# Two of the seven products of a Strassen-like layer made by halves again, in two of three chunks

## The chip, the cores and the metric

The kernel runs on one core of one Trainium2 chip. The metric is the device time of one execution in microseconds (us). The kernel before takes 889.53 us, the median of 3 runs (889.41 to 889.66). The profile is of one such execution; its span is 887.6 us.

The engines are named as the profile names them: PE is TensorE (matmul), PEld its weight load, DVE is VectorE, ACT is ScalarE, POOL is GpSimd, SP is SyncE. A queue name such as SPq or POOLq stands for the transfers that this engine issues.

## The reference

The reference is an attention with a mask, followed by a feed-forward part with a squared ReLU. The change touches the feed-forward part only.

```python
# attention: batch 4, heads 8, sequence 768, head_dim 64
attn_out = hash_attention(q, k, v, proj)           # masked softmax, cut here
# bridge: (B,H,S,D) -> (B*S, H*D) = (3072, 512)
x = attn_out.transpose(0, 2, 1, 3).reshape(B * S, H * D)
# feed-forward: w_in (512, 2048), w_out (2048, 512), all f32
h = x @ w_in
r = np.maximum(h, 0.0)
g = r * r
out = g @ w_out
```

## The kernel before

The kernel works in two parts. The first, up to about 335 us, does the attention and writes its result to `x_all`. The second does the feed-forward part in 3 chunks of 1024 tokens. In each chunk there is a first layer (`h = x @ w_in` and the gate) and a second layer (`g @ w_out`, called `project`).

Both layers save matmuls by a scheme of Strassen's kind. A product of 2 x 2 blocks, which would need eight block products, is made of seven: four of the seven factors on each side are sums or differences of blocks, and the results are added up. The first layer applies the scheme once. A unit is 2 x 128 rows of hidden features (blocks `b11`, `b12`, `b21`, `b22`), and there are 8 units a chunk. The second layer applies the scheme twice, which makes 49 products with factors called `leaf`. All factors on the weight side are prepared earlier and kept in device memory: `w_in_7` for the first layer, `w_out_49` for the second.

The seven products, shared by both layers. Each `add` is a group of `n` matmuls into an accumulator in PSUM; three of the outputs share an accumulator, whose running value is copied out between the products:

```python
def product(n, w, at, bt, c11, c12, c21, c22, hook=None):
    acc = [ps_m.tile([P, 512], FP32, name=f"acc{i}")[:, 0:w] for i in range(3)]
    ...                                   # add(), keep(): keep copies acc out by ScalarE
    add(0, at(0), bt["11"], True, False)
    one = keep(0, "one")
    add(1, at(1), bt["21"], True, True)
    if hook:
        hook()
    c11(acc[1], one)
    add(0, at(4), bt["t2"], False, False)
    two = keep(0, "two")
    add(2, at(3), bt["t1"], True, False)
    five = keep(2, "five")
    add(0, at(5), bt["t3"], False, False)
    three = keep(0, "three")
    add(2, at(6), bt["22"], False, True)
    c12(acc[2], two)
    c22(three, five)
    add(0, at(2), bt["t4"], False, True)
    c21(acc[0])
```

The first layer. `HN` is 512 columns, `NFT // 2` is 2 tiles of the contraction:

```python
def load_unit(n, pool=p_i):               # 7 factors of a unit, 896 KB, on SP's queue
    r = n % NR
    w_unit[n] = pool.tile([P, 7, NFT // 2, P], FP32, name="w_unit", bufs=2 ...)
    nc.sync.dma_start(out=w_unit[n], in_=w_in_7[r])

def hidden(i, r):
    ...
    def gate(out):
        def put(one, two=None):
            h = p_r.tile([P, HN], FP32, name="h", bufs=NH)
            if two is None:
                nc.scalar.copy(out=h, in_=one)
            else:
                nc.vector.tensor_tensor(out=h, in0=one, in1=two, op=ALU.add)
            nc.vector.scalar_tensor_tensor(
                out=out[:, r], in0=h, scalar=0.0, in1=h, op0=ALU.max, op1=ALU.mult
            )
        return put
    product(NFT // 2, HN, lambda a: lambda f: w[:, a, f], bt,
            gate(b11), gate(b12), gate(b21), gate(b22))
```

The second layer, cut to its order. `QN` is 256 columns, `NQ` is 4. Seven outer products `k`, each made by a `product` of seven inner ones with 4 matmuls of 256 columns. The operand `y21` of an inner seventh product is made in place by `hook`, on DVE. Sums of the next outer factor are made ahead by `inner_sums`:

```python
for k in range(7):
    ...
    def hook():
        y21 = b[:, NQ:NR, 0:QN]
        minus(y21, y21, t2)
        if k + 1 < 7 and k not in (1, 3):
            inner_sums(k + 1)
    product(NQ, QN, a_with_load, bt, ..., hook)
    if k == 0 and i + 1 < NCHUNK:
        load_x(i + 1)                      # 2048 KB on POOL's queue
    if k in (3, 4) and i + 1 < NCHUNK:
        sum_x(i + 1, 2 * k - 5); sum_x(i + 1, 2 * k - 4)
    if k == 0:                             # k == 2 alike, with b_t and b21
        for h in range(2): minus(b11[...], b22[...], b_t[...])
        inner_sums(2)
```

The main loop, cut. `peak` is a maximum over 768 elements a row of `q` and `k` that the kernel needs once; its 32 pieces are spread over chunks 2 and 3:

```python
for i in range(NCHUNK):
    for r in range(NR):
        hidden(i, r)
        minus(b_t[:, r], b12[:, r], b11[:, r])
        ...                                # work on w_out's factors in chunk 1
        load_unit(i * NR + r + ...)
        for n in range(2):
            m = 2 * ((i - 1) * NR + r) + n
            if m >= 0: peak(m)
            if 0 <= m + 2 < NPK: load_peak(m + 2)
        if r >= THEN[-1]:                  # r >= 5
            inner_sums(0, slice(r - NQ if r > THEN[-1] else 0, r - NQ + 1))
        minus(b12[:, r], b22[:, r], b12[:, r])
    project(i)
```

Of the kernel before, what the change touches and what calls it, by code (L numbers as in the profile page):

```python
# [8 lines left out]
FP32 = mybir.dt.float32  # L9
# [25 lines left out]
def kernel(  # L35
# [10 lines left out]
    nc = tc.nc  # L46
# [34 lines left out]

    HF, HD, NR, NQ = DFF // 2, DM // 2, NFF // 2, NFF // 4
    w_in_7 = p_d.tile([NR, P, 7, NFT // 2, P], FP32, name="w_in_7")
    w_in_21 = p_d.tile([P, NFT // 2, HF], FP32, name="w_in_21")
    w_out_1 = p_d.tile([P, NFF, DM], FP32, name="w_out_1")
    w_out_49 = p_d.tile([7, P, 7, NQ, P], FP32, name="w_out_49")
# [110 lines left out]
    def put_factor(n, c, t):  # L197

        for f in range(NFT // 2):
            rs = t[:, f].rearrange("p (r c) -> p r c", c=P)  # L200
            nc.sync.dma_start(
                out=w_in_7[c // P:c // P + rs.shape[1], :, n, f].rearrange("r p c -> p r c"), in_=rs
            )


# [298 lines left out]

    def sums_a(a11, a12, a21, a22, s1, s2, s3, s4):
        nc.vector.tensor_tensor(out=s1, in0=a21, in1=a22, op=ALU.add)
        nc.vector.tensor_tensor(out=s3, in0=a11, in1=a21, op=ALU.subtract)
        nc.vector.tensor_tensor(out=s2, in0=s1, in1=a11, op=ALU.subtract)  # L510
        nc.vector.tensor_tensor(out=s4, in0=a12, in1=s2, op=ALU.subtract)

    def minus(out, in0, in1):
        nc.vector.tensor_tensor(out=out, in0=in0, in1=in1, op=ALU.subtract)  # L514
# [28 lines left out]

    w_unit = {}

    def load_unit(n, pool=p_i):

        if n < NCHUNK * NR and n not in w_unit:
            r = n % NR
            w_unit[n] = pool.tile([P, 7, NFT // 2, P], FP32, name="w_unit", bufs=2 if pool is p_i else 1)  # L550
            nc.sync.dma_start(out=w_unit[n], in_=w_in_7[r])

    def sum_x(i, n):

# [18 lines left out]
    with tc.manual_schedule():  # L573
# [191 lines left out]
                op0=ALU.mult, op1=ALU.is_gt,  # L765
            )

        def hidden(i, r):

            x, t_x = xs[i]  # L770
            lo, hi = slice(0, HN), slice(HN, NCH)
            w = w_unit.pop(i * NR + r)
            bt = {
                "11": lambda f: x[:, f, lo], "21": lambda f: x[:, 2 + f, lo],
                "22": lambda f: x[:, 2 + f, hi], "t4": lambda f: x[:, f, hi],
            }
            for n in range(3):
                bt[f"t{n + 1}"] = lambda f, n=n: t_x[n][:, f]

            def gate(out):  # L780
                def put(one, two=None):
                    h = p_r.tile([P, HN], FP32, name="h", bufs=NH)
                    if two is None:
                        nc.scalar.copy(out=h, in_=one)
                    else:
                        nc.vector.tensor_tensor(out=h, in0=one, in1=two, op=ALU.add)  # L786
                    nc.vector.scalar_tensor_tensor(  # L787
                        out=out[:, r], in0=h, scalar=0.0, in1=h, op0=ALU.max, op1=ALU.mult
                    )
                return put  # L790

            product(
                NFT // 2, HN, lambda a: lambda f: w[:, a, f], bt, gate(b11), gate(b12), gate(b21),
                gate(b22),
            )

        def parts_t(b, n):

            lo, hi = slice(0, QN), slice(QN, HN)
            return b[:, n, lo], b[:, n, hi], b[:, NQ + n, lo], b[:, NQ + n, hi]  # L800


        OUTER = (0, b11), (5, b12), (3, b_t), (6, b22), (1, b21), (4, b11), (2, b_t)
# [3 lines left out]
        def inner_sums(k, n=slice(0, NQ)):  # L807

            if k not in tens:
                tens[k] = [p_y.tile([P, NQ, QN], FP32, name=f"t{m}", bufs=2) for m in range(2)]  # L810
            t1, t2 = (t[:, n] for t in tens[k])
            b = OUTER[k][1]
            at = slice(NQ + n.start, NQ + n.stop)
            y11, y12, y21, y22 = b[:, n, 0:QN], b[:, n, QN:HN], b[:, at, 0:QN], b[:, at, QN:HN]
            minus(t1, y12, y11)
            minus(t2, y22, t1)
            minus(y12, y22, y12)
# [3 lines left out]
        def load_leaf(n, early=False):  # L821
            if n < 49:
                k, m = divmod(n, 7)
                m = LEAVES[m]
                leaves[k, m] = p_y.tile([P, NQ, P], FP32, name="leaf", bufs=NLEAF)
                queue = nc.sync if early else nc.scalar
                queue.dma_start(out=leaves[k, m], in_=w_out_49[OUTER[k][0], :, m])
# [55 lines left out]
        def project(i):  # L883
# [54 lines left out]
            def fourth(n, one, two):  # L938
                add_to(out_block(1, 0, n), block(W, n), whole(one, two))
                close(1, 0, n)  # L940

            uses = first_, seventh, fifth, third, second, sixth, fourth
            for k in range(7):
                b = OUTER[k][1]
                t1, t2 = tens.pop(k)
                at = lambda m, k=k: lambda n: leaves[k, m][:, n]
                bt = {
                    "11": lambda n: b[:, n, 0:QN], "21": lambda n: b[:, NQ + n, 0:QN],
                    "22": lambda n: b[:, NQ + n, QN:HN], "t1": lambda n: t1[:, n],
                    "t2": lambda n: t2[:, n], "t3": lambda n: b[:, n, QN:HN],  # L950
                    "t4": lambda n: b[:, NQ + n, 0:QN],
                }

                def hook():
                    y21 = b[:, NQ:NR, 0:QN]
                    minus(y21, y21, t2)
                    if k + 1 < 7 and k not in (1, 3):
                        inner_sums(k + 1)

                counted = []  # L960

                def a_with_load(m, k=k):
                    load_leaf(7 * k + len(counted) + NLEAF - 2)
                    counted.append(m)
                    return at(m)

                use = uses[k]
                product(
                    NQ, QN, a_with_load, bt, lambda *p: use(0, *p), lambda *p: use(1, *p),
                    lambda p: use(2, p, None), lambda *p: use(3, *p), hook,  # L970
                )
                if k == 0 and i + 1 < NCHUNK:
                    load_x(i + 1)
                if k in (3, 4) and i + 1 < NCHUNK:
                    sum_x(i + 1, 2 * k - 5)
                    sum_x(i + 1, 2 * k - 4)
                if k == 5 and i + 1 == NCHUNK:
                    guard()
                if k == 0:

                    for h in range(2):
                        at_h = slice(h * NQ, (h + 1) * NQ)
                        minus(b11[:, at_h], b22[:, at_h], b_t[:, at_h])
                    inner_sums(2)
                if k == 2:

                    for h in range(2):
                        at_h = slice(h * NQ, (h + 1) * NQ)
                        minus(b_t[:, at_h], b21[:, at_h], b11[:, at_h])
                    inner_sums(4)  # L990
# [41 lines left out]
        load_unit(2, p_1)  # L1032
        load_rows(1)
        for i in range(NCHUNK):
            for r in range(NR):
                hidden(i, r)
                minus(b_t[:, r], b12[:, r], b11[:, r])
                if i == 0 and r in WHEN:
                    sums_out(WHEN.index(r))
                if i == 0 and r in THEN:  # L1040
                    m = THEN.index(r)
                    sums_out_49(m)
                    if m + 2 < NQ:
                        load_rows(m + 2)
                if i == 0 and r == THEN[-1]:
                    p_1s.close()
                    p_y = fast.enter_context(tc.tile_pool(name="p_y", bufs=1, reuse_waits="tile"))
                load_unit(i * NR + r + (3 if i == 0 and r < 2 else 2))
                if r == NR - 2:
                    for n in range(NLEAF - 2):  # L1050
                        load_leaf(n, i == 0)
                for n in range(2):
                    m = 2 * ((i - 1) * NR + r) + n
                    if m >= 0:
                        peak(m)
                    if 0 <= m + 2 < NPK:
                        load_peak(m + 2)
                if r >= THEN[-1]:
                    inner_sums(0, slice(r - NQ if r > THEN[-1] else 0, r - NQ + 1))
                minus(b12[:, r], b22[:, r], b12[:, r])  # L1060
            if i == NCHUNK - 1:
                tops()
            project(i)
# [5 lines left out]
def general(tc, slow, ident, w_in_7, w_in_21, w_out_1, q, k, v, proj, out_v):  # L1069
# [19 lines left out]
    with ExitStack() as stack:  # L1089
# [9 lines left out]
        with tc.If(flag > 0), ExitStack() as inner:  # L1099
            const = inner.enter_context(tc.tile_pool(name="g_const", bufs=1))  # L1100
            w_out = const.tile([P, NFF, DM], FP32, name="g_w_out")
            nf, nr = NFT // 2, NFF // 2
            for n, f, c in (0, 0, 0), (1, nf, 0), (2, nf, nr):
                for i in range(nf):
                    nc.sync.dma_start(
                        out=w_in_d[c:c + nr, :, f + i], in_=w_in_7[:, :, n, i]
                    )
# [192 lines left out]
```

## Time and profile before

| what | value |
|---|---|
| time, median of 3 | 889.53 us (889.41 to 889.66) |
| span of the profiled execution | 887.6 us |
| mean granted PE clock | 0.997 of full speed |
| HBM traffic | 119.28 MB read, 38.01 MB written |
| `w_unit<-w_in` loads | 24 of 896 KB, median 4.7 us to landing |
| `leaf<-w_out` loads on ACT's queue | 142 of 256 KB, median 2.9 us to landing |

How to read it. The page gives the busy time of each engine, the span in 40 slices, the DMA queues, the chain of work that ended last (followed back from the last instruction), and groups of instructions by source line. A group names the tile that is written and those that are read, `acc<-x,w_unit`, with the shape and the count. A timeline line has the start, the duration, the engine, the source line and the operands, and in brackets how long the engine was idle before and who released it. A matmul in f32 appears as two records, and its modelled end can lie after the start of the next one, so the spacing of the starts tells more than the durations. Line 697 is the matmul in `add`, line 514 the helper `minus`.

### The profile page before, as it was taken

How to read it: one execution, taken by the hardware profiler on the slowest of the kernel's cores; microseconds unless marked ns; L12 is line 12 of the kernel's file. 1: busy time of each engine (PE TensorE's matmuls, PEld its weight loads, DVE VectorE, ACT ScalarE, POOL GpSimd, SP SyncE). 2: the span in 40 equal slices, each digit the busy share in tenths (PEclk: the TensorE clock that was granted, in tenths of full speed). 3: DMA queues.
4: the chain of work that ended last, by engine and by line, in shares of the span. 5: the costliest groups of instructions: out<-in, count | busy, mean ns of one | idle time of the engine just before them, and what ended most of it. 6: DMA issues, size and time to landing. Idle time of an engine off the chain costs nothing.

```text
span 887.6 us, 11727 instructions
## 1 busy us (share of the span) xinstructions
PE 873.3 (98%) x4268; PEld 502.7 (57%) x4268; DVE 715.8 (81%) x994; ACT 376.0 (42%) x609; POOL 91.5 (10%) x148
## 2 busy tenths in 40 slices
PE   8999999999999999999999999999999999999996
PEld 3444444444444444444688854445888644458885
DVE  5899999999999998888779955568789556778875
ACT  5988888888888852222111112222111122221110
POOL 2000000000000001554000111112000111100002
PEclk9999999999999999999999999999999999999998
DMA  9677779898878536999855834447757444444565
GB/s 182 130 150 134 196 184 202 167 277 198 167 154 213 155 114 222 293 264 292 312 169 152 190 85 137 132 152 259 255 162 176 74 154 154 153 132 145 163 172 104
DMA packets 220032, 158.14 MB, mean 178 GB/s; under 512 B 163808, under 2 KB 180704, under 8 KB 219968
## 3 DMA queue, kind: packets, MB, share of 16 engines
q1 hardware_dynamic: 186848, 84.04, 39.3%
q10 hardware_dynamic: 22384, 37.76, 14.1%
q0 software_dynamic: 10736, 35.53, 13.2%
q8 instruction: 35, 0.57, 0.3%
q14 instruction: 29, 0.24, 0.1%
HBM read 119.28 MB, written 38.01 MB: 177 GB/s over the span
## 4 chain that ended last, share of the span: by engine, by line
PE 93%; DVE 4%; ACT 1%; DMA 1%; issue 1%; ACTq 0%; DVEq 0%
PE acc L697 60%; PE st L394 17%; PE xo L436 13%; PE tot L455 2%; PE hash L344 1%; DVE total L426 1%; DMA k_nat<-in_k_dram 1%; ACT e L411 1%; ACT bits L354 1%; DVE peaks L738 0%; DVE b L787 0%; DVE h L786 0%; DMA w_in<-s_in 0%; DVE t L514 0%; DVE out_piece L177 0%
## 5 line engine op out<-in xcount | busy, mean ns | idle before, releaser
L697 PE MATMUL acc<-x,w_unit 128*128 128x512 f32 x384 | 169.4, 593 | 0.0
L411 ACT ACTIVATE e<-st 128x1024 f32<-128x1024 f32 x192 | 145.2, 810 | 46.9 <-PE st L394 42.7
L394 PE MATMUL st<-feat,feat 64*128 64x512 f32 (+1 forms) x768 | 150.5, 484 | 0.0
L436 PE MATMUL xo<-e,v_nat 128*64 128x512 f32 (+1 forms) x768 | 134.8, 492 | 0.0
L697 PE MATMUL acc<-b,leaf 128*128 128x256 f32 x600 | 132.9, 380 | 0.0
L697 PE MATMUL acc<-t_x,w_unit 128*128 128x512 f32 x288 | 127.6, 593 | 0.0
L697 PEld LDWEIGHTS acc<-x,w_unit 128*128 128x128 f32 x384 | 73.0, 190 | 90.5 <-issue 88.5
L697 PEld LDWEIGHTS acc<-b,leaf 128*128 128x128 f32 x600 | 114.3, 190 | 16.5 <-issue 1.4
L426 DVE TENSOR_TENSOR total<-total,e 128x1536 f32<-128x1536 f32 x61 | 107.1, 1756 | 4.3
L436 PEld LDWEIGHTS xo<-e,v_nat 128*64 128x64 f32 x768 | 51.4, 136 | 82.4 <-issue 75.2
L697 PEld LDWEIGHTS acc<-t_x,w_unit 128*128 128x128 f32 x288 | 54.8, 190 | 69.0 <-issue 66.8
L394 PEld LDWEIGHTS st<-feat,feat 64*128 64x128 f32 x768 | 66.1, 188 | 33.7 <-issue 24.1
L786 DVE TENSOR_TENSOR h<-acc,two 128x512 f32<-128x512 f32 x24 | 16.6, 691 | 83.7 <-PE acc L697 83.6
L704 ACT COPY two<-acc 128x512 f32<-128x512 f32 (+1 forms) x45 | 21.9, 486 | 132.6 <-PE acc L697 132.6
L697 PE MATMUL acc<-t,leaf 128*128 128x256 f32 x336 | 76.5, 380 | 0.3 <-DVE t L514 0.3
L354 ACT ACTIVATE bits<-hash,lifts 32x384 bf16<-32x384 f32 x120 | 68.6, 572 | 3.2 <-issue 1.3
L697 PEld LDWEIGHTS acc<-t,leaf 128*128 128x128 f32 x336 | 63.8, 190 | 9.5 <-DVE t L514 1.1
L704 ACT COPY one<-acc 128x512 f32<-128x512 f32 (+1 forms) x45 | 21.9, 486 | 111.8 <-PE acc L697 78.3
L787 DVE SCALAR_TENSOR_TENSOR b<-h 128x512 f32<-128x512 f32 x96 | 64.3, 690 | 2.5
L394 PE MATMUL st<-bits,bits 64*128 64x256 bf16 (+1 forms) x384 | 63.3, 326 | 1.8 <-ACT e L411 1.4
L697 PE MATMUL acc<-b_t,leaf 128*128 128x256 f32 x240 | 53.8, 380 | 0.0
L697 PEld LDWEIGHTS acc<-b_t,leaf 128*128 128x128 f32 x240 | 45.6, 191 | 6.1
(130 smaller groups left out, 864.3 us busy)
## 6 DMA issues: line engine op xcount, KB each, us to landing
leaf<-w_out ACTq DMA_DIRECT2D x142, 256.0 KB, 2.9
w_unit<-w_in SPq DMA_DIRECT2D x24, 896.0 KB, 4.7
raw<-in_moe_w_in_dram SPq DMA_DIRECT2D x16, 512.0 KB, 5.6
raw<-in_moe_w_out_dram SPq DMA_DIRECT2D x16, 512.0 KB, 4.3
w_out<-sums POOLq DMA_DIRECT2D x16, 448.0 KB, 6.8
v_nat<-in_v_dram SPq DMA_DIRECT2D x16, 384.0 KB, 4.9
x_all<-x_t SPq DMA_DIRECT2D x16, 384.0 KB, 3.0
x<-x_all POOLq DMA_DIRECT2D x3, 2048.0 KB, 12.2
```

What stands on the lines that cost most here:

```text
L344: nc.tensor.matmul(out=banks[g * NR_B:(g + 1) * NR_B, h, 0:HS], lhsT=projs[rows], rhs=feat[pr, w][rows, c * HS:(c + 1) * HS], start=True, ...
L354: nc.scalar.activation(out=t[h * D:h * D + NR_B, c * HS:(c + 1) * HS], in_=hashed[pr, w][at, h, 0:HS], func=ACTF.Sign, scale=HUGE, bias=li ...
L394: nc.tensor.matmul(out=st[:, h, 0:hi - lo], lhsT=src[pr, 1][rows, key], rhs=src[pr, 0][rows, lo:hi], start=first, stop=not first,)
L411: nc.scalar.activation(out=e[:, :, lo:hi], in_=sts[i][:, :, 0:hi - lo], func=ACTF.Exp, scale=scale)
L426: nc.vector.tensor_tensor(out=totals[pr], in0=totals[pr], in1=weights[pr, kt][:, :, 0:S], op=ALU.add)
L436: nc.tensor.matmul(out=xo[h * D:(h + 1) * D, lo:hi], lhsT=nat[pr, "v_nat"][:, h, kt * D:(kt + 1) * D], rhs=weights[pr, kt][:, h, lo:hi], s ...
L455: nc.tensor.matmul(out=tot[g * 32:(g + 1) * 32, 0:HS], lhsT=ones, rhs=src[:, h, c * HS:(c + 1) * HS], start=src is srcs[0], stop=src is sr ...
L697: nc.tensor.matmul(out=acc[to], lhsT=a(i), rhs=b(i), start=first and i == 0, stop=last and i == n - 1, skip_group_check=True,)
L704: nc.scalar.copy(out=t, in_=acc[of])
L786: nc.vector.tensor_tensor(out=h, in0=one, in1=two, op=ALU.add)
L787: nc.vector.scalar_tensor_tensor(out=out[:, r], in0=h, scalar=0.0, in1=h, op0=ALU.max, op1=ALU.mult)
```

## The change

In the second and third chunk, the units of the first layer are taken in pairs (units n and n + 4). Five of the seven products stay as they are for each unit. The other two, those with factors 1 and 2 of each unit, are joined over the pair: two units by two tiles of the contraction are a 2 x 2 block on the weight side, and the 512 columns are cut in two on the other side. Each of the two is then made by the scheme again: seven inner products of one matmul of 256 columns, in place of two units by two matmuls of 512 columns. This is for fewer matmul columns: 7 x 256 in place of 8 x 256 for each.

The weight factors for it, `w_in_49`, are made from `w_in_7` during the second layer of the first chunk, with loads and stores on POOL's queue and sums on DVE. The order of the factors in `w_in_7` changes so that the five that stay lie together. The matmuls of an inner product stand between those of the outer ones, so that the copy of an accumulator has time. The partial results go to snapshot tiles in place of output tiles that are free then (`o`), and the inner factors go to tiles of the second layer that are free then (`sum0` to `sum3`, `t0`, `t1`). The maxima `peak` move to the end of a unit's work, behind the inner sums.

```diff
+    w_in_49 = p_d.tile([NQ, P, 2, 7, P], FP32, name="w_in_49")
...
+    PLACE = 0, 5, 6, 1, 2, 3, 4
...
-            r = n % NR
+            r = order(n)                       # units 0,4,1,5,2,6,3,7 from chunk 2 on
             w_unit[n] = pool.tile([P, 7, NFT // 2, P], FP32, name="w_unit", ...)
-            nc.sync.dma_start(out=w_unit[n], in_=w_in_7[r])
+            m = 7 if n < NR else 5
+            nc.sync.dma_start(out=w_unit[n][:, 0:m], in_=w_in_7[r, :, 0:m])
...
+        def factor_units(n):                   # second layer of chunk 1, k = 0..3
+            src = [new_h()... for _ in range(2)]
+            for j in range(2):
+                nc.gpsimd.dma_start(out=src[j], in_=w_in_7[j * NQ + n, :, 5:7])
+            sums = [new_h()... for _ in range(2)]
+            sums_a(...)                        # 4 DVE operations of 256 elements a row
+            for lo, hi, t in (...):            # 4 stores
+                nc.gpsimd.dma_start(out=w_in_49[n, :, :, lo:hi], in_=t)
+
+        def load_inner(i, n):                  # 2 loads of 448 KB a pair, on SP's queue
+            ...
+        def sums_inner(i):                     # 8 DVE operations of 256, once a chunk
+            ...
+        def inner_steps(i, n, j):
+            ...
+            def step_0():
+                a0, a1 = (ps_m.tile([P, 512], FP32, name="acc1")[:, 0:QN] for _ in range(2))
+                mul(a0, 0, y11, True, False)
+                nc.scalar.copy(out=one, in_=a0)
+                mul(a1, 1, y21, True, True)
+                hs[0] = new_h()
+                nc.vector.tensor_tensor(out=hs[0][:, 0:QN], in0=a1, in1=one, op=ALU.add)
+            def step_1():
+                hs["a2"] = ps_t.tile([P, 512], FP32, name="acc3")[:, 0:QN]
+                mul(hs["a0"], 4, t[:, 1], False, False)
+                nc.scalar.copy(out=two, in_=hs["a0"])
+                mul(hs["a2"], 3, t[:, 0], True, False)
+                nc.scalar.copy(out=five, in_=hs["a2"])
+            def step_2():
+                mul(hs["a0"], 5, t3, False, False)
+                nc.scalar.copy(out=three, in_=hs["a0"])
+                mul(hs["a2"], 6, y22, False, True)
+                nc.vector.tensor_tensor(out=hs[0][:, QN:HN], in0=hs["a2"], in1=two, op=ALU.add)
+                hs[1] = new_h()
+                nc.vector.tensor_tensor(out=hs[1][:, QN:HN], in0=three, in1=five, op=ALU.add)
+            def step_3():
+                mul(hs["a0"], 2, t[:, 2], False, True)
+                nc.scalar.copy(out=hs[1][:, 0:QN], in_=hs["a0"])
+            def put(unit, out, other):
+                h = hs[unit]
+                nc.vector.tensor_tensor(out=h, in0=h, in1=other, op=ALU.add)
+                gated(out, h)
+
+        def hidden_pair(i, n, half):
+            ...
+            add(0, 0, "11", True, False)
+            one = keep(0, "one")
+            if half: now[0][4](1, b11[:, r], one)
+            else:    steps[0]()
+            add(2, 3, "t1", True, False)
+            five = keep(2, "five")
+            steps[1 - half]()
+            add(0, 4, "t2", False, False)
+            two = keep(0, "two")
+            steps[2 - half]()
+            if half == 0: put(0, b11[:, r], one)
+            add(2, 6, "22", False, True)
+            gate_sum(b12[:, r], acc[2], two)
+            steps[3 - half]()
+            if half: put(0, b21[:, n], now["three"])
+            add(0, 5, "t3", False, True)
+            three = keep(0, "three")
+            gate_sum(b22[:, r], three, five)
+            if half:
+                steps[3]()
+                put(1, b21[:, r], three)
...
             for k in range(7):
+                if i == 0 and k < NQ:
+                    factor_units(k)
+                if k == 6 and more:
+                    load_inner(i + 1, 0)
...                                             # in hook():
+                    if k == 6 and more:
+                        sums_inner(i + 1)
...                                             # main loop
-            for r in range(NR):
-                hidden(i, r)
+            for s in range(NR):
+                r = order(i * NR + s)
+                if i == 0: hidden(i, r)
+                else:      hidden_pair(i, s // 2, s % 2)
...
+                if i == 0 and r >= THEN[-1]:
+                    inner_sums(0, ...)
+                if i > 0 and s % 2:
+                    inner_sums(0, slice(s // 2, s // 2 + 1))
+                minus(b12[:, r], b22[:, r], b12[:, r])
                 for n in range(2):             # peak() and load_peak(), as before
                     ...
-                if r >= THEN[-1]:
-                    inner_sums(0, ...)
-                minus(b12[:, r], b22[:, r], b12[:, r])
```

## The prediction

> **What bounds the kernel now.** I read the page's busy table and the chain of waits first, then the groups by line, then the busy time in six stretches that I cut at the chunk stages, and last the timeline of TensorE (PE), VectorE (DVE) and GpSimd (POOL) where the first chunk's second layer begins.
>
> ```profile
> PE 873.3 (98%) x4268; PEld 502.7 (57%) x4268; DVE 715.8 (81%) x994; ACT 376.0 (42%) x609; POOL 91.5 (10%) x148
> ...
> PE 93%; DVE 4%; ACT 1%; DMA 1%; issue 1%; ACTq 0%; DVEq 0%
> PE acc L697 60%; PE st L394 17%; PE xo L436 13%; PE tot L455 2%; PE hash L344 1%; DVE total L426 1%; DMA k_nat<-in_k_dram 1%; ACT e L411 1%; ACT bits L354 1%; DVE peaks L738 0%; DVE b L787 0%; DVE h L786 0%; DMA w_in<-s_in 0%; DVE t L514 0%; DVE out_piece L177 0%
> ```
>
> PE is 93% of the chain, and line 697, the products of both layers of the feed-forward part, is 60% of it. So a matmul less in that part is time less, as long as PE stays fed. The stretches (first and second layer of chunks 1, 2, 3; columns: length, busy PE, weight load, DVE, ACT, POOL, clock, DMA share, GB/s):
>
> ```profile
> 335.00:431.00 96.00, 96.00 (x224) 42.41 (x224) 77.84 (x113) 22.82 (x39) 35.54 (x40) 1.00 0.87 274
> 431.00:515.60 84.60, 84.60 (x393) 74.62 (x392) 70.74 (x99) 11.76 (x31) 5.94 (x9) 1.00 0.66 191
> 515.60:611.90 96.30, 96.30 (x226) 42.63 (x225) 60.23 (x93) 22.82 (x39) 14.91 (x28) 1.00 0.44 143
> 611.90:696.00 84.10, 83.94 (x389) 73.76 (x388) 71.57 (x99) 11.75 (x31) 8.05 (x13) 1.00 0.69 202
> 696.00:792.70 96.70, 96.70 (x230) 43.35 (x229) 60.74 (x93) 22.82 (x39) 14.92 (x28) 1.00 0.42 133
> ```
>
> The reader is to see three things. PE has no gap in a first layer (96.3 of 96.3 us). There DVE is busy 60 of 96 us, so it has room. In a second layer DVE is busy 71 of 84.6 us, so it has little. The start-to-start times in PE's timeline give the unit costs:
>
> ```profile
> 427.63 3.60 PE L697 MATMUL acc<-x,w_unit 128*128 128x512 f32 x8
> 431.06 3.62 PE L697 MATMUL acc<-b,leaf 128*128 128x256 f32 x16
> 434.51 3.62 PE L697 MATMUL acc<-t,leaf 128*128 128x256 f32 x16
> ```
>
> An f32 matmul leaves two records. 8 records of 512 columns start 3.43 us before the next group: 0.43 us a record, 0.86 a matmul. 16 records of 256 columns: 3.45 us, 0.2157 a record, 0.43 a matmul. Half the columns cost half the time, although every record loads its own weights (190 ns, hidden).
>
> **What the Trainium skill says.** "TensorE: Matmul & The Clock Gate", section "Back-to-back issue gap", gives 262 cycles for 256 columns and 518 for 512, so halving the width loses about 1%; the trace agrees (2 x 0.2157 = 0.431 against 0.430). "Perfetto Trace Analysis", section "Identifying the Most-Contended Engine", warns that busy matmul time is a poor measure, which is why I use the spacing of starts and not the busy share. "VectorE: DVE Perf Modes", section on the TRN2 errata, has (N+151)/0.96 ns for an f32 tensor_tensor: 691 ns for 512 elements and 424 for 256; the trace has 684 to 691 and 418 to 425. "DMA: Bandwidth & Descriptors", section "Two DMAs through the same engine are not ordered", says that within one queue of one DMA engine descriptors start in order; no run shows it yet, and one step below rests on it.
>
> **The change part by part.**
>
> 1. PE, first layer of chunks 2 and 3. A pair of units makes two of its seven products by halves. Removed: 2 units x 2 products x 2 K tiles = 8 matmuls of 512 columns, 8 x 0.860 = 6.88 us. Added: 2 x 7 matmuls of 256 columns, 14 x 0.4314 = 6.04 us. A gain of 0.84 us a pair; 4 pairs x 2 chunks: 6.7 us. That is the whole of what PE can gain, 0.75% of 889.53.
>
> 2. DVE in those stages. Per unit: one more add of 512 (the fourth output was a ScalarE copy and is now an add), 0.69, and three adds of 256, 3 x 0.42 = 1.26; 1.95 us. Times 8: 15.6 on 60.2 = 76 us, in a stage of 96.3 - 3.35 = 93 us: 82%. It fits.
>
> 3. ACT there: five copies of 256 (372 ns each in the groups) in place of one of 512 (585 ns): +1.28 us a unit, 22.8 + 10.2 = 33 of 93 us. It fits.
>
> 4. Waits inside a pair. An inner accumulator is copied out between its products, so its next matmul must wait for that copy. In the code's order at least one outer product (2 x 0.86 = 1.72 us) lies between; a copy takes 0.37 after a semaphore. I expect no gap. The single buffer of `acc3` and the shared snapshot tiles `o` are read by DVE adds; walking DVE's order through both halves, DVE is up to 5 to 6 us behind at a pair's start (a gate 1.3, the second unit's gate 1.3, b_t 0.6, inner sums 1.1, b12 0.6, two maxima 1.7), and the next overwrite comes some 5 us after an add that stood ahead of all these. No gap.
>
> 5. Transfers. Per pair 2 x 640 + 2 x 448 = 2176 KB in place of 2 x 896 = 1792. The DMA share there is 0.42 to 0.44: hidden.
>
> 6. Reordering. The last inner sums now stand before the two maxima. In the kernel before, PE waits for `t` at the start of each of the last two second layers (releaser DVE t: the chain leaves PE at 610.48 and comes back at 617.00); PE's start-to-start shows about 0.3 us lost in the second chunk. The fourth output adds 0.7 us ahead, the maxima give back 1.7. Gain about 0.4 us in both together.
>
> 7. Preparing the inner factors, in the second layer of chunk 1. Ahead of each of the first four products, two 256 KB loads on POOL's queue, four DVE adds of 256 (4 x 0.40 = 1.6 us) and four stores. DVE is the issue. It works in program order, and the lines around the second product (PE from 443.15) are:
>
> ```profile
> 442.36 4.49 DVE L514 TENSOR_TENSOR b<-b,b_t 128x2048 f32<-128x2048 f32 x2
> 446.77 1.22 DVE L514 TENSOR_TENSOR t<-b_t 128x1024 f32<-128x1024 f32 x1
> 448.02 1.22 DVE L514 TENSOR_TENSOR t<-b_t,t 128x1024 f32<-128x1024 f32 x1
> 449.16 1.22 DVE L514 TENSOR_TENSOR b_t<-b_t 128x1024 f32<-128x1024 f32 x1
> 450.30 1.22 DVE L514 TENSOR_TENSOR b<-b,t 128x1024 f32<-128x1024 f32 x1
> ```
>
> The last line makes the operand of that product's seventh part. It ends at 451.52. PE starts that part after six of 1.727 us: 443.15 + 10.36 = 453.5. The slack is 2.0 us. The new sums of the first block (about 1.6 us from 435.3 on) are mostly swallowed by an idle 1.39 us of DVE at 441.7; 0.2 us goes on. Those of the second stand right before the line at 450.30, for 1.6 us. That takes the slack to 0.2 us if their data is there.
>
> It may not be. The chunk's 2 MB load `x` is on the same POOL queue:
>
> ```profile
> 431.52 0.75 POOL L541 DMA_DIRECT2D x<-x_all  x1 [13.55 <-PE acc L697]
> ```
>
> The list of transfers gives its size and the time to landing:
>
> ```profile
> x<-x_all POOLq DMA_DIRECT2D x3, 2048.0 KB, 12.2
> ```
>
> Now the first block's stores precede it, and they wait for sums that end at about 436.9; `x` is issued at about 438.2 and lands 12.2 us later, at 450.4. The second block's two loads are issued behind it, and if they start in order they land 2 to 3 us after it, at about 453. Then the sums run to 454.6, the operand is ready at 455.8, and PE stands for 455.8 - 453.5 = 2.3 us. At the fourth product the same walk (its operand ready at 475.69 before, needed at 467.32 + 10.36 = 477.7, slack 2.0, less 1.6) leaves 0.4 us: 0.2 us of stall at most in my centre. Third product: slack 5.5 us, no stall. In the last product of chunks 1 and 2, eight more DVE operations of 256 (3 us) meet an idle 2.89 us at 514.2: hidden.
>
> Sum: 889.53 - 6.7 - 0.4 + 2.3 + 0.2 = 884.9 us.
>
> **The rivals.** (a) Everything is hidden and the second block's data comes in time (the queue interleaves its transfers): no stall, 889.5 - 7.1 = 882.4. For it: PE ran gapless before. (b) DVE late in the second layer costs more: `x` lands later because leaf loads share the DMA engines (256 KB each 1.73 us), and each later product inherits the delay; 5 to 6 us of stall, 888. For it: DVE is gapless from 442 to 451 and from 466 to 477. (c) The inner products themselves stall: PE waits in each half for a copy or a snapshot, 0.4 us in 16 halves makes 6.4 us, 891. For it: single-matmul groups with a semaphore each are new. Against it: the 1.72 us of outer work between, and that groups of four in the second layer show no cost at their seams (8.80 us for 40 records). (d) DVE becomes the bound in chunks 2 and 3: that needs 93 us, the sum is 76. Unlikely.
>
> **Range and chances.** Centre 884.9. Without the stall 882.4, with it doubled 887.4; 8 in 10 between 882.4 and 888.0. Faster by over 2% would need 17.8 us, against a whole gain of 7: 0.01. Slower by over 2% needs a stall in every half of 1.5 us: 0.02.
>
> **What would show it.** PE's span from the first to the last matmul of a first layer in chunks 2 and 3: 93 us for 96.3 (step 1 right, and no waits in pairs). A PE gap released by a DVE subtraction near 453 us, with DVE's new sums waiting on a DMA just before (step 7). Chunk 3's second layer unchanged at about 84.2 to 84.6 us. If PE shows gaps at the 256-column matmuls of the first layer, released by ACT copies or DVE adds, step 4 is wrong; if the gap at 453 is missing, the queue did not hold the loads back.

## The result

The changed kernel takes 883.38 us, the median of 6 runs (883.2 to 884.64); the kernel before, beside it, 889.6 us. The ratio is 0.9932, with a 95% interval of 0.9919 to 0.9945: faster by 0.7%. The prediction was 884.9 us, in a range of 882.4 to 888.0.

The page of the changed kernel, busy times and chain:

```profile
PE 866.7 (98%) x4364; PEld 519.5 (59%) x4364; DVE 756.3 (86%) x1096; ACT 391.9 (44%) x673; POOL 107.2 (12%) x172
...
PE 94%; DVE 2%; ACT 1%; DMA 1%; issue 1%; ACTq 0%; DVEq 0%
PE acc L708 40%; PE st L396 17%; PE acc L927 16%; PE xo L438 13%; PE acc L880 5%; PE tot L457 2%; PE hash L346 1%; DVE total L428 1%; DMA k_nat<-in_k_dram 1%; ACT e L413 1%; ACT bits L356 1%; DMA w_in<-s_in 0%; DVE out_piece L179 0%; DVE power L171 0%; ACT small L160 0%
```

The old line 697 is now three: 708 (`product`), 927 (outer products of a pair) and 880 (inner products). Together they are 61% of a shorter chain, and DVE has fallen from 4% to 2% of it: the subtractions and maxima that were listed in the chain before (`DVE peaks`, `DVE b`, `DVE h`, `DVE t`) are no longer listed. DVE as a whole works 40 us more (756.3 against 715.8), and none of the lines that do this new work is listed in the chain.

The same stretches as before the change (first and second layer of chunks 1, 2, 3):

```profile
335.00:431.23 96.23, 96.23 (x224) 42.48 (x225) 78.08 (x113) 22.87 (x39) 37.61 (x44) 1.00 0.88 279
431.23:516.91 85.68, 85.08 (x393) 74.31 (x392) 78.92 (x122) 11.76 (x31) 19.47 (x30) 1.00 0.83 254
516.91:609.91 93.00, 93.00 (x274) 51.84 (x273) 73.74 (x126) 30.78 (x71) 14.96 (x28) 1.00 0.49 159
609.91:694.66 84.75, 84.75 (x394) 74.40 (x393) 76.48 (x110) 11.65 (x32) 8.08 (x13) 1.00 0.70 208
694.66:787.50 92.84, 92.84 (x273) 51.68 (x273) 73.60 (x126) 30.78 (x71) 14.97 (x28) 1.00 0.48 152
```

PE is gapless in the first layers of chunks 2 and 3, which are shorter by over 3 us: 160 records of 512 columns at 0.4291 us and 112 of 256 at 0.2159 (the mean spacing of starts there) make the whole 92.84 us of the stage. The one stretch that is longer than before is the second (85.68 us, PE busy 85.08). The exact stages follow from the start of the first matmul of each stage in PE's timeline; the last column runs to the closing transposes:

| us | layer 1, c1 | layer 2, c1 | layer 1, c2 | layer 2, c2 | layer 1, c3 | layer 2, c3 |
|---|---|---|---|---|---|---|
| before | 96.34 | 84.61 | 96.26 | 85.03 | 96.13 | 86.26 |
| changed | 96.33 | 85.68 | 92.84 | 84.74 | 92.84 | 85.99 |
| difference | 0.0 | +1.07 | -3.42 | -0.29 | -3.29 | -0.27 |

They add up to -6.2 us, the difference of the two spans (887.6 and 881.4).

Where the second layer of chunk 1 loses time. DVE around its second product, in the changed kernel:

```profile
449.34 1.22 DVE L519 TENSOR_TENSOR b_t<-b_t 128x1024 f32<-128x1024 f32 x1
451.39 0.43 DVE L513 TENSOR_TENSOR h<-h 128x256 f32<-128x256 f32 x1 [0.83 <-DMA h<-w_in]
451.73 0.42 DVE L514 TENSOR_TENSOR h<-h 128x256 f32<-128x256 f32 x1
452.06 0.42 DVE L515 TENSOR_TENSOR h<-h 128x256 f32<-128x256 f32 x1
452.52 0.42 DVE L516 TENSOR_TENSOR h<-h 128x256 f32<-128x256 f32 x1
452.86 1.22 DVE L519 TENSOR_TENSOR b<-b,t 128x1024 f32<-128x1024 f32 x1
```

And PE at the same place and at the fourth product:

```profile
450.23 3.62 PE L708 MATMUL acc<-b,leaf 128*128 128x256 f32 x16
454.18 1.96 PE L708 MATMUL acc<-b,leaf 128*128 128x256 f32 x8 [0.34 <-issue]
...
474.98 3.62 PE L708 MATMUL acc<-b,leaf 128*128 128x256 f32 x16
478.85 5.42 PE L708 MATMUL acc<-b,leaf 128*128 128x256 f32 x24 [0.26 <-issue]
```

16 records take 3.45 us, so the seventh part was due at 450.23 + 3.45 = 453.68. It starts at 454.18, just after the operand is made (452.86 + 1.22 = 454.08): 0.50 us late. At the fourth product: 474.98 + 3.45 = 478.43, and it starts at 478.85: 0.42 us late. The record behind each of the two is 0.07 us late as well; that makes the 1.07 us. The profile writes "issue" here and not DVE; the times tell the releaser. DVE's 0.83 us of waiting for the load precede the first of the two.

### The profile page after: what moved, and what is told of

The parts are those of the page before. It is cut to its first block, busy times and chain, and to the rows that moved or that the text cites. A ratio compares the mean times of both kernels' runs of the same rounds, so it can differ in the third digit from the quotient of the medians.

```text
span 881.4 us, 12164 instructions
## 1 busy us (share of the span) xinstructions
PE 866.7 (98%) x4364; PEld 519.5 (59%) x4364; DVE 756.3 (86%) x1096; ACT 391.9 (44%) x673; POOL 107.2 (12%) x172
## 4 chain that ended last, share of the span: by engine, by line
PE 94%; DVE 2%; ACT 1%; DMA 1%; issue 1%; ACTq 0%; DVEq 0%
PE acc L708 40%; PE st L396 17%; PE acc L927 16%; PE xo L438 13%; PE acc L880 5%; PE tot L457 2%; PE hash L346 1%; DVE total L428 1%; DMA k_nat<-in_k_dram 1%; ACT e L413 1%; ACT bits L356 1%; DMA w_in<-s_in 0%; DVE out_piece L179 0%; DVE power L171 0%; ACT small L160 0%
## 5 line engine op out<-in xcount | busy, mean ns | idle before, releaser
L927 PE MATMUL acc<-t_x,w_unit 128*128 128x512 f32 x192 | 90.2, 592 | 0.0
L927 PE MATMUL acc<-x,w_unit 128*128 128x512 f32 x128 | 60.1, 592 | 0.0
L708 PE MATMUL acc<-x,w_unit 128*128 128x512 f32 x128 | 56.6, 594 | 0.0
L927 PEld LDWEIGHTS acc<-t_x,w_unit 128*128 128x128 f32 x192 | 36.5, 190 | 28.9 <-issue 26.8
L715 ACT COPY two<-acc 128x256 f32<-128x256 f32 (+1 forms) x29 | 12.5, 432 | 87.7 <-PE acc L708 72.2
L715 ACT COPY one<-acc 128x256 f32<-128x256 f32 (+1 forms) x29 | 12.5, 432 | 85.9 <-PE acc L708 47.6
L396 PEld LDWEIGHTS <-bits 64*128 64x128 bf16 x384 | 23.4, 93 | 41.6 <-issue 37.9
```

Of the source, the lines that this page charges most:

```text
L396: nc.tensor.matmul(out=st[:, h, 0:hi - lo], lhsT=src[pr, 1][rows, key], rhs=src[pr, 0][rows, lo:hi], start=first, stop=not first,)
L708: nc.tensor.matmul(out=acc[to], lhsT=a(i), rhs=b(i), start=first and i == 0, stop=last and i == n - 1, skip_group_check=True,)
L715: nc.scalar.copy(out=t, in_=acc[of])
L927: nc.tensor.matmul(out=acc[to], lhsT=w[:, PLACE[a], f], rhs=bt[b](f), start=first and f == 0, stop=last and f == NFT // 2 - 1, skip_group_ ...
```

## The experiments

Each was run beside the kernel before. The stage times are taken as in the table above.

**e1, the reordering alone, in the kernel before.**

```diff
-   (two maxima)   inner_sums(0, ...)   minus(b12, ...)
+   inner_sums(0, ...)   minus(b12, ...)   (two maxima)
```

> The kernel before with one thing changed: the two maxima move behind the inner sums and b12. Theory: the second layers of chunks 2 and 3 lost 0.4 and 0.0-0.4 us at their start (85.03 us in chunk 2 against 84.61 in chunk 1) and get 84.7 to 84.8 us; about 0.5 us faster, 889.1 against 889.6. Rival (the order of the maxima is without effect): 889.6, and 85.0 us again in the second layer of chunk 2.

Measured: 888.61 us against 889.57, ratio 0.9989 (0.9982 to 0.9996). The second layers of chunks 2 and 3 take 84.61 and 85.82 us (85.03 and 86.26 before). Both waits for `t` are gone: 0.42 and 0.44 us. PE at the first of them, in the kernel before and in e1:

```profile
617.00 2.42 PE L697 MATMUL acc<-t,leaf 128*128 128x256 f32 x10 [0.16 <-DVE t L514]
```

```profile
615.21 3.62 PE L697 MATMUL acc<-t,leaf 128*128 128x256 f32 x16
```

In the kernel before, the 16 records on `t` are broken by a wait after the sixth; in e1 they run through. So a gain of 0.9 us, nearly twice the 0.5 expected, has nothing to do with fewer products.

**e2, the changed kernel with the old order.**

```diff
-   inner_sums(0, ...)   minus(b12, ...)   (two maxima)
+   (two maxima)   inner_sums(0, ...)   minus(b12, ...)
```

> The changed kernel with the old order, maxima ahead of the inner sums. Theory: with pairs, DVE has one more add of 0.7 us ahead of t, so the old order makes t 1.8 us later: PE's wait at the start of the second layers of chunks 2 and 3 grows from 0.14 to about 1.9 us each, 883.4 + 3.5 = 887 us. Rival (the reordering is worth only what it is worth in the kernel before, 0.5 us): 883.9.

Measured: 887.27 us, ratio 0.9975 (0.9963 to 0.9986). PE at the start of the second layer of chunk 2:

```profile
616.48 2.43 PE L708 MATMUL acc<-t,leaf 128*128 128x256 f32 x10 [1.59 <-DVE t L519]
```

The two stages take 86.57 and 87.68 us in place of 84.74 and 85.99: 3.5 us lost, as the theory had it. The reordering is worth 0.9 us in the old kernel and 3.5 us in the new one. Without it the change would have brought 2.3 us in place of 6.2.

**e3, the factors made but not used.**

```diff
-   hidden_pair(i, s // 2, s % 2)      # chunks 2, 3; loads of 640 KB + inner factors
+   hidden(i, r)                       # as before; whole loads of 896 KB
-   load_inner(...); sums_inner(...)
```

> The changed kernel without the pairs: chunks 2 and 3 make all seven products as before, with whole loads of 896 KB; the inner factors are still prepared in the second layer of chunk 1 but never used, and the new order of the maxima stays. Theory: preparation costs 1.07 us in that stage (85.68 against 84.61), the order gives 0.5: 889.6 + 1.07 - 0.5 = 890.2. Rival (the 1.07 us come from the preparation of the pairs' operands, the eight sums and the loads of factors at the end, not from making the factors): 889.1.

Measured: 890.92 us, ratio 1.0012 (1.0003 to 1.002), so 2.3 us more than e1, which differs by the preparation and by the order of the factors in `w_in_7`. About 0.4 us of that lies outside the span of the instructions (the time is 2.18 us longer than the span here and 1.78 in e1, by the medians). The rival falls: making the factors costs time by itself. The profiled execution is the longest of the 12 (892.28 us); in it the second layer of chunk 1 takes 87.27 us, and PE waits there for leaves too:

```profile
449.13 1.99 PE L708 MATMUL acc<-t,leaf 128*128 128x256 f32 x8 [0.41 <-DMA leaf<-w_out]
451.37 3.76 PE L708 MATMUL acc<-b,leaf 128*128 128x256 f32 x16 [0.25 <-DMA leaf<-w_out]
456.32 1.96 PE L708 MATMUL acc<-b,leaf 128*128 128x256 f32 x8 [1.20 <-issue]
```

```profile
453.53 0.42 DVE L513 TENSOR_TENSOR h<-h 128x256 f32<-128x256 f32 x1 [2.92 <-DMA h<-w_in]
```

By the spacing of the starts, the first two groups are 0.57 and 0.51 us late, behind leaves. The third, the seventh part of the second product, is 1.50 us late: DVE waited 2.92 us for the second block's load, so its operand was ready only at 456.22. Loads of `leaf` took 6.0 us to land (median) between 431 and 455 us, against 4.7 in the changed kernel. The DMA engines are busy in both (a share of 0.80 over the stage here, 0.83 in the changed kernel). The cost of the preparation is not one fixed number.

**e4, the inner products in one block.**

```diff
-   steps[0]() ; add(...) ; steps[1]() ; add(...) ; steps[2]() ; add(...) ; steps[3]()
+   for step in steps: step()          # between two outer products, once in each half
```

> The changed kernel with the seven inner products one after the other in each half, not between outer ones. Theory: each next product on the first inner accumulator then waits for ScalarE's copy with only one matmul of 0.43 us beside it, 0.3 us three times in 16 halves, 14 us: 897, and the gain is gone. Rival (PE takes such waits for nothing because copies overlap): 883.4 to 885.

Measured: 900.09 us, ratio 1.011 (1.0094 to 1.0127). The first layers of chunks 2 and 3 take 100.49 and 100.50 us in place of 92.84, 0.96 us more in each of 16 halves. PE's products and weight loads and ACT's copies in one half:

```profile
518.84 1.03 PE L880 MATMUL acc<-x,sum 128*128 128x256 f32 x4
...
519.52 0.38 ACT L887 COPY o<-acc 128x256 f32<-128x256 f32 x1
519.95 0.73 PEld L880 LDWEIGHTS acc<-t,sum 128*128 128x128 f32 x4 [0.49 <-ACT o L887]
519.95 1.13 PE L880 MATMUL acc<-t,sum 128*128 128x256 f32 x4
...
520.68 0.37 ACT L896 COPY o<-acc 128x256 f32<-128x256 f32 x1 [0.79 <-PE acc L880]
521.11 0.73 PEld L880 LDWEIGHTS acc<-x,sum 128*128 128x128 f32 x4 [0.43 <-ACT o L896]
521.11 1.13 PE L880 MATMUL acc<-x,sum 128*128 128x256 f32 x4
522.27 0.30 PEld L880 LDWEIGHTS acc<-t,sum 128*128 128x128 f32 x2 [0.43 <-ACT o L902]
```

Two matmuls (4 records) take 0.86 us, so the pair from 518.84 is done at 519.70, and the next starts at 519.95; that one is done at 520.81, and the next starts at 521.11; that one is done at 521.97, and the last starts at 522.27. These three gaps of 0.25 to 0.30 us are 0.85 of the 0.96 us. The gap column of PE shows nothing, because a matmul's modelled end lies beyond the true one; the weight loads beside it name the releaser, the copy. The theory's 14 us were 15.3. The second layers of chunks 2 and 3 take 0.6 us more each as well (85.37 and 86.62); the theory had nothing there. The rival falls.

**e5, the sums moved to later products.**

```diff
-   if i == 0 and k < NQ: factor_units(k)          # ahead of products 0, 1, 2, 3
+   if i == 0 and k in (0, 4, 5): factor_units(k - 2 if k else 0)
...                                                # and behind product 1: factor_units(1)
```

> The changed kernel with the preparation of the second block of factors moved behind the second product, and that of the third and fourth to the fifth and sixth product. Theory: the 1.07 us come from sums that stand right before an operand that PE needs 2 us later; moved to where DVE is idle or has 4 us of slack, the second layer of chunk 1 takes 84.6 us again and the kernel 882.3. Rival (the loads and stores on the queues themselves slow the leaf loads or DVE): 85.2 to 85.7 us, 883 or more. Second rival (the slack of the later products is used up): a new wait at the sixth or seventh product.

Measured: 884.42 us, ratio 0.9937 (0.9923 to 0.995); the second layer of chunk 1 takes 86.40 us. Not better. The stall at the second product is gone, but the last two products have new ones: the seventh part of the last product was due at 511.08 + 3.45 = 514.53 us and starts at 515.79. The first layer behind it takes 93.13 us, 0.29 more than in the changed kernel. DVE's timeline shows why the parts are late:

```profile
511.08 3.62 PE L708 MATMUL acc<-b_t,leaf 128*128 128x256 f32 x16
515.79 1.97 PE L708 MATMUL acc<-b_t,leaf 128*128 128x256 f32 x8 [1.10 <-issue]
```

```profile
496.44 0.42 DVE L513 TENSOR_TENSOR h<-h 128x256 f32<-128x256 f32 x1
499.91 0.42 DVE L514 TENSOR_TENSOR h<-h 128x256 f32<-128x256 f32 x1 [3.05 <-DMA out_dram<-h]
```

The fourth block's sums need a tile `h`, and from the fifth product on these tiles hold outputs on their way to memory. DVE waits 3.05 us for such a store, and everything behind it is late. The theory's first half held, the second rival was nearer, and the cause was one that neither named: a shared buffer.

**e6, the load of x on another queue.**

```diff
-   nc.gpsimd.dma_start(out=x, in_=x_all[...])
+   (nc.sync if i else nc.gpsimd).dma_start(out=x, in_=x_all[...])
```

> The changed kernel with the 2 MB load of x for chunks 2 and 3 on SP's queue in place of POOL's. Theory: the second block's loads landed only 12 us after their issue because they stood behind x in the queue; now they land in 3 to 4 us, DVE's wait of 0.83 us at 451 us goes, and PE's stall of 0.50 us at 453.7 goes; the stall of 0.42 us at the fourth product stays: 882.9. Rival (the DMA engines are just full then): loads take 9 us or more as before and the stall stays.

Measured: 882.52 us (881.83 to 884.46), ratio 0.9923 (0.9909 to 0.9936). The second layer of chunk 1 takes 85.04 us. POOL's timeline in the changed kernel, the loads of the second block and the store that waits for them:

```profile
437.91 0.95 POOL L546 DMA_DIRECT2D x<-x_all  x1
438.67 1.28 POOL L833 DMA_DIRECT2D h<-w_in  x2
450.60 0.68 POOL L842 DMA_DIRECT2D w_in<-h  x1 [10.65 <-DMA h<-w_in]
```

And with `x` on SP's queue:

```profile
437.81 1.39 POOL L833 DMA_DIRECT2D h<-w_in  x2
446.44 0.68 POOL L842 DMA_DIRECT2D w_in<-h  x1 [7.24 <-DMA h<-w_in]
```

The loads are there 4 us earlier. They are still slow (8.3 and 8.8 us, against a median of 6.2 for all eight), so part of the rival is true: the DMA engines are full (a share of 1.0 from 437.8 to 447.2 us). But DVE now finds them in place: the second block's sums start at 450.39 with no wait, and PE's stall at the second product is gone.

The edit changed two things, though. On POOL's queue `x` stood behind the first block's stores, which wait for DVE, and was issued at 437.91; on SP's queue it is issued at 431.72 and lands at 444.34 in place of 449.38. So e6 does not tell whether another queue or the earlier issue brought the loads forward. They still land behind `x`, at 446.2 and 447.2.

About 0.4 us are left in the stage, and not where the theory had them:

```profile
445.10 1.59 PEld L708 LDWEIGHTS acc<-b,leaf 128*128 128x128 f32 x8 [0.36 <-DMA leaf<-w_out]
...
474.76 8.80 PE L708 MATMUL acc<-b,leaf 128*128 128x256 f32 x40
483.39 3.62 PE L708 MATMUL acc<-t,leaf 128*128 128x256 f32 x16
```

By PE's starts, 0.23 us are lost at 445.10, for a leaf, and 0.20 at 447.05, where no releaser is named. At the fourth product 40 records take 8.63 us, 0.216 each: that stall is gone too. Its sums stand where they stood, but DVE's wait for the third block's loads ends at 460.15 in place of 460.99, and DVE keeps this lead. So the stall at the fourth product came down the same chain from the late loads of the second block.

**e7 and e8, more work for DVE in the pairs.**

```diff
-   minus(b_t[:, r], b12[:, r], b11[:, r])
+   for _ in range(1 if i == 0 else 3):            # e8: 5
+       minus(b_t[:, r], b12[:, r], b11[:, r])     # the same result each time
```

> The changed kernel with DVE's subtraction for b_t done three times in place of once in each unit of chunks 2 and 3 (2 x 0.65 us more of DVE work a unit). Theory: DVE has room in the pairs, 73.7 + 10.4 = 84 of 93 us, so the first layers stay at 92.84 us; at the start of the second layer t comes 1.2 us later, so 1.0 to 1.3 us each are lost there: 885.7. Rival (DVE is already the bound in the pairs by its order): first layers of 95 us or more, 888 and up.

Measured: 886.12 us, ratio 0.9962 (0.9949 to 0.9976). The first layers of chunks 2 and 3 take 92.84 and 92.85 us, with DVE busy 82.75 us of that in chunk 2. The second layers lose 1.44 us each (86.18 and 87.42), the wait for `t`, a little more than the 1.0 to 1.3 expected. As the theory had it: there is room for DVE within the pairs, and none at their end.

> The same with five subtractions in place of one (4 x 0.65 us more a unit). Theory: 73.7 + 20.8 = 94.5 us of DVE work against 92.84: DVE becomes the bound, the first layers take 94 to 97 us, and 2.5 us are lost at the start of each second layer: 890 to 897. Rival (room is larger than the busy time says): first layers stay at 92.9.

Measured: 910.01 us, ratio 1.0221 (1.0206 to 1.0237). DVE is the bound, but the time shows up elsewhere than expected: the first layers take 94.21 us, only 1.4 us more, and the second layers 96.62 and 98.00 us, 12 us more. DVE in a late pair, from one inner sum to the same one of the next pair:

```profile
577.38 0.42 DVE L890 TENSOR_TENSOR h<-acc,o 128x256 f32<-128x256 f32 x1
...
602.90 0.41 DVE L890 TENSOR_TENSOR h<-acc,o 128x256 f32<-128x256 f32 x1
```

25.5 us of DVE work without a gap, for a pair that takes PE 23.2. PE ran ahead of DVE (its first layer is only 1.4 us longer), so DVE fell behind, and PE pays when the second layer needs `t`. And it pays twice:

```profile
615.63 1.99 PE L708 MATMUL acc<-b,leaf 128*128 128x256 f32 x8 [2.03 <-DVE h L890]
617.46 1.46 PE L708 MATMUL acc<-t,leaf 128*128 128x256 f32 x6
625.89 4.63 PE L708 MATMUL acc<-t,leaf 128*128 128x256 f32 x10 [6.98 <-DVE t L519]
630.32 9.11 PE L708 MATMUL acc<-b,leaf 128*128 128x256 f32 x40
```

The 10 records after the gap of 7 us take 4.43 us from start to start, 0.44 each in place of 0.216. The granted clock is 0.50 of full speed from 624.1 to 630.9 us, and 1.00 before and after. The same wait in chunk 3 (6.98 us) ends in the same way: 10 records in 4.42 us. The expected 890 to 897 missed this.

**e9 and e10, another version, and the changed kernel beside it.** e9 is e6 with the fourth block ahead of the fifth product, where no output store holds a tile yet:

```diff
-   if i == 0 and k < NQ: factor_units(k)
+   if i == 0 and k in (0, 1, 2, 4): factor_units(min(k, NQ - 1))
```

> The changed kernel with x on SP's queue as in the run before, and the fourth block of factors prepared ahead of the fifth product in place of the fourth (the others stay). Theory: what is left of the loss in the second layer of chunk 1 (85.04 against 84.61 us) is the fourth block's sums ahead of an operand needed at once; ahead of the fifth product DVE has 4 us of slack and no output store holds a tile yet, so the stage takes 84.61 us and the kernel 882.1. Rival (any later sums eat the slack of the seventh product): a stall of 0.3 us or more at the sixth or seventh product, 882.5 or more.

Measured: 882.33 us (882.27 to 882.86), ratio 0.992 (0.9907 to 0.9934). The second layer of chunk 1 takes 84.81 us, with no stall at any seventh part. That is within 0.2 us of the kernel before in this stage. But the theory's reason does not hold: e6 had no stall at the fourth product that could have gone. What e9 still loses (0.20 us) it loses between 445 and 447 us, as e6 did. By their times e6 and e9 cannot be told apart (881.83 to 884.46 and 882.27 to 882.86), so that the fourth block's move gained anything is not shown. Nor is a cost to be seen. The operand behind the moved sums:

```profile
485.40 1.22 DVE L519 TENSOR_TENSOR b<-b,t 128x1024 f32<-128x1024 f32 x1
```

This operand is ready at 486.6 and needed at about 490.1 (product five starts at 479.70; six parts of 1.727 us): 3.5 us of slack are left.

> The changed kernel itself, beside the run before on the same chip: how much its loss in the second layer of chunk 1 varies. Theory: first layers of 92.84 us, and 1.0 to 1.8 us lost in the second layer of chunk 1, as the other runs with the same preparation had; 883.4 to 884.0, so 1.1 to 1.8 us above the run before. Rival (the differences between these versions are noise of the whole execution): the same time as the run before.

Measured: 884.06 us (883.4 to 884.43), ratio 0.9935 (0.9921 to 0.9948), 1.7 us above e9 on the same chip; the two ranges of runs do not overlap, while the two intervals of the ratio do. So the loss in this stage is not noise, and `x` issued early on SP's queue takes it away. Here DVE waits 1.99 us for the second block's load, and the second layer of chunk 1 takes 86.66 us:

```profile
449.45 1.22 DVE L519 TENSOR_TENSOR b_t<-b_t 128x1024 f32<-128x1024 f32 x1
452.66 0.42 DVE L513 TENSOR_TENSOR h<-h 128x256 f32<-128x256 f32 x1 [1.99 <-DMA h<-w_in]
```

Over the six profiles with this same preparation and pairs' code after it (the changed kernel, e2, e4, e7, e8, e10), the stage takes 85.68, 85.96, 86.07, 86.32, 86.40 and 86.66 us. In e10 0.37 us of this are waits near 452 us, the longest of them for a leaf; in the other five all of the loss stands at the second and fourth products.

## Why the prediction was right, point by point

The mechanisms stood; one term of the sum, the stall in the second layer of chunk 1, was too large.

1. PE's matmuls: 6.7 us predicted, 3.42 + 3.29 = 6.71 us measured. Half the columns did cost half the time, to 0.6% (2 x 0.2159 against 0.4291; the prediction quotes about 1%), also for single matmuls with a wait each. That the sum fits to 0.01 us is luck: by the records a stage gains 64 x 0.4291 - 112 x 0.2159 = 3.28 us, and the other 0.13 us of chunk 2 are a small wait near 603 us of the kernel before that the changed one doesn't have. The prediction's 0.860 a matmul was rounded up from 0.858.
2. DVE in the pairs: 76 us predicted, 73.7 measured, of 92.84. Room confirmed by e7, its limit by e8, rival (d).
3. ACT: 33 us predicted, 30.8 measured.
4. Waits inside a pair: none predicted, none measured. e4 shows that this is the interleaving's doing and not a matter of course; the rival (c) that I had at 891 us was real for another order.
5. Transfers in the pairs: the DMA share rose to 0.48 to 0.49; hidden, as predicted.
6. The reordering: 0.4 us predicted for what it leaves, 0.29 + 0.27 = 0.56 measured. That these are near is partly luck. The waits of the kernel before were 0.42 and 0.44 us (e1), not 0.3 in one chunk; and the sign "chunk 3's second layer unchanged at about 84.2 to 84.6 us" was misread: 84.10 was a stretch of chunk 2's second layer cut 1 us too early, and chunk 3's took 86.26 us before and 85.99 after. The working was thin: I compared the old kernel with the new one and did not ask what the pairs would have cost without it. e2 says 3.5 us.
7. The preparation: this is the term that was too large. Predicted were stalls of 2.3 us at the second product and 0.2 at the fourth; in this profile they are 0.50 and 0.42, in all 1.07 us of the stage. At the second product the place and the chain (`x`, then loads, then sums, then operand, then PE) were as predicted, and so was the order in the queue, which rested on "DMA: Bandwidth & Descriptors" of the Trainium skill, section "Two DMAs through the same engine are not ordered": in all eight profiles with `x` on POOL's queue ahead of the second block's loads, the three land in the order of their issue, the loads 0.9 to 1.2 and 1.9 to 2.1 us after `x`. So the interleaving of rival (a) did not happen, though its 882.4 us, the sum without the stall, is what e6 and e9 reached. The size of the step "the loads land at about 453 us" was off: `x` took 11.5 us and not 12.2, and the loads landed at 450.3 and 451.4, so that DVE waited 0.83 us and not 2.5. At the fourth product the prediction counted only the sums standing there, and left 0.4 us of slack. It missed that DVE would come 0.8 us later there: its step `b_t<-b,b` starts 0.05 us after the product's first matmul (468.12 against 468.07), where before it started 0.78 us ahead of it (466.54 against 467.32), and from its wait of 4.19 us for the third block's loads, which ended at 460.99, to 478.66 DVE had no gap. In the other profiles DVE waited up to 2.06 us for the second block (e8), and the stage lost 1.35 to 2.05 us. The landing time varies from execution to execution, and I took it as a fixed 12.2 us and added 2 to 3 for what stands behind. The changed kernel was again at 884.06 in e10, so the distance to 884.9 is this term.

The eight sums at the end of a chunk are hidden, as predicted: PE has no gap around 511 to 517 us.

What stays open: what sets the landing time of `x` from one execution to the next, 11.5 to 12.6 us in the seven profiles with pairs and 13.5 in e3; the loads behind it keep their distance. Leaf loads share the DMA engines, and they are slower in e3, which loads whole units, but no run took them away. Open too is what the other queue alone is worth, without the earlier issue.

## What to carry to other kernels

When one engine has no gaps, a saving on it is worth what its records say, here to 0.13 us of 6.7; what is uncertain is the work that pays for it, and where in program order of another engine it stands. Ask for each added operation which operand is made right behind it, and how long before its use: 2 us of slack were gone after 1.6 us of sums and one late load. A small load issued behind a large one in the same queue landed as late as the large one (11.6 and 12.2 us in place of 5.1 to 6.1); and tiles that are free in one stage may be held by stores in the next.

## What was not expected of the hardware

Two 256 KB loads issued right after a 2 MB load on POOL's queue took 11.6 and 12.2 us to land in the changed kernel, and 13.8 and 14.3 in e3; the other six such loads of the changed kernel took 5.1 to 6.1 us. With the large one on SP's queue, and issued 6.2 us earlier, the longest was 8.8 us.

After 7 us without work PE ran 10 records at 0.44 us each in place of 0.216 (e8, in both chunks); the granted clock is 0.50 from 624.1 to 630.9 us, and it fell 1.8 us before PE's work went on. This wait cost 2.3 us more than its length. The wait of 2.03 us before it shows no such fall: the eight records behind it take 1.83 us.

DVE operations of 256 elements that do not depend on each other start 0.34 us apart although each lasts 0.42; one that depends on the one before starts 0.45 us after it (the four sums from 451.39 us on, shown above: the fourth takes the result of the third).
